# Float64 weights joined to float32 by integer operations instead of TensorE sums, and a planner with other step lengths and one booking for VectorE and GpSimd

## The chip, the cores and the metric

The kernel runs on one core of one Trainium2 chip. The metric is the device time of one execution in microseconds, lower is better; a kernel is run several times and its median is given. A profile is one further execution, recorded instruction by instruction.

## The reference

Three blocks follow each other. First an attention: `q` has 12288 rows of 128, `kv` is a 384 x 32 field of rows of 128 that is averaged over 4 x 4 patches to 768 rows and multiplied by `w_sr` (128 x 128); the same 768 rows are keys and values.

```
kv_pool = kv.reshape(B, H // r, r, W // r, r, C).mean(axis=(2, 4))
k = v = kv_pool.reshape(B, -1, C) @ w_sr
s = scale * (q @ k.transpose(0, 2, 1));  s = s - s.max(-1)
a = np.exp(s);  a /= a.sum(-1) + 1e-09;  x = a @ v
x = g1(x @ w_in1) @ w_out1      # g1(h) = h if h > 0 else exp(h) - 1
x = g2(x @ w_in2) @ w_out2      # g2(h) = max(0.01 h, h)
```

Both layers have 128 x 2048 weights in and 2048 x 128 weights out. The four weight matrices come as float64, everything else as float32.

## The kernel before

*Products.* Every large product is done with float32r operands in three passes (`mm3`, L88 to L91): a number is split in a head `hi` (the value rounded to float32r) and a tail `lo` (what is left), and hi x hi, hi x lo and lo x hi are summed in PSUM. So every operand needs a head, mostly made by ScalarE or GpSimd, and a tail, mostly a subtraction on VectorE.

*Stages.* The 12288 rows go in 24 chunks of 512. For each chunk, four tiles of 128 rows go through the attention: `scores` (TensorE), `largest` (VectorE, L343), `expo` (ScalarE, L350), `invert` (VectorE, L358 and L359), `norm` (GpSimd, L369), then the transposition of the probabilities, `head_e` (ScalarE, L414) and `tail_e` (VectorE, L418). In the first two chunks TensorE transposes (`turn_early`, L409); later ones go through DRAM (`send`, `fetch`, two transfers on SP) and a VectorE transpose (L398). `values` (L429) makes the chunk's attention output in 18 matmuls, `head_x` and `tail_x` (L437) split it. Then come the two layers in units of 256 of the 2048 hidden columns, 8 units a chunk and layer: `up` into a PSUM place, the activation, `tail` (L496), `down` into a sum `py`. Ten units of layer one run alone; then units of layer one and layer two alternate. At the start `kv` is loaded in 12 transfers and pooled (`column_sums` on VectorE, L283; `row_sums` on TensorE, L292).

*The weights.* The four matrices are cut into 16 parts of 128 x 512. Each is loaded as pairs of 32-bit words (`load_w`) into one of two `ws` buffers and made into a head and a tail that stay in SBUF (`w_parts`). Before the change a part goes through nine steps: ScalarE takes the absolute value of the high word read as float32 (`w_abs`, L197); GpSimd bounds it (`w_bound`, L201); VectorE shifts it left by 3 bits (`w_shift`, L208), which makes the float64 exponent a float32 one, puts sign and top bit back (`w_sign`, L215) and takes the power of two alone (`w_power`, L222). ScalarE rounds to the head (`w_head`, L228), VectorE scales the low word by the power of two (`w_b`, L233). Then TensorE sums in a PSUM place the float32 value times the identity (L240), minus the head (L241) and plus the low word's share (L242), and ScalarE copies that sum out as the tail (`w_tail`, L245), which frees the place. Four parts are due early, the others six units ahead of the unit that uses them.

*PSUM.* Three places of 128 x 1024 (`ps`) serve scores, early transposes, attention output, up products and weight sums in turn; two more are the sums `py`. A place is held from the first matmul of its use to the end of the last reader.

*The order of work.* Nothing is written in program order by hand. `step` registers each operation with its engine, an estimated length, what it comes after and a due key; `take` and `give` register buffers and PSUM places. A greedy planner then goes through time: of all steps that can begin it takes the one that begins first, ties within 0.25 us going to the lower key, and emits it. `LATE` is the delay after which another engine sees a result. The order in which a step is emitted is the order on its engine's queue; the engines work their queues in order and wait on semaphores.

Of the kernel before, what the change touches and what calls it, by code (L numbers as in the profile page):

```python
# [36 lines left out]
TOP = struct.unpack("f", struct.pack("I", 0x47EFFFFF))[0]  # L37
LEAST = struct.unpack("f", struct.pack("I", 0x38000000))[0]
# [3 lines left out]
def pooled_attention_elu_leaky_kernel(  # L42
# [55 lines left out]
    plus = const.tile([P, P], F32R, name="plus")  # L98
    minus = const.tile([P, P], F32R, name="minus")
# [23 lines left out]
    wt_p = pool("wt", 1)  # L123
# [61 lines left out]
    def w_parts(i):  # L185

        k, p = wjobs[i]  # L190
# [58 lines left out]

# [9 lines left out]
    nc.scalar.activation(out=plus, in_=ident, func=AF.Copy)  # L259
    nc.scalar.activation(out=minus, in_=ident, func=AF.Copy, scale=-1.0)  # L260
# [274 lines left out]
    def step(engine, length, do, after, key, size=0):  # L535
# [5 lines left out]
        steps.append((engine, length, do, [a for a in after if a is not None], key, size))  # L541
# [37 lines left out]
    for i in range(NL):  # L579
# [3 lines left out]
        cs = step(DVE, 0.7, lambda i=i: column_sums(i), [ld], key + 1)  # L583
        rs = step(PE, 0.5, lambda i=i: row_sums(i), [cs, previous], key + 1)
# [17 lines left out]
    for i, (k, p) in enumerate(wjobs):  # L602
# [29 lines left out]
    tq = step(DVE, 0.7, lambda: turn_q(0), first_q[:1], begin + 12)  # L632
# [259 lines left out]
```

## Time and profile before

| what | value |
| --- | --- |
| median of 3 runs | 1345.92 us (1345.49 to 1346.61) |
| span of the profiled execution, first to last instruction | 1343.9 us |
| what the median has beyond that span | 2.0 us |
| instructions in the profile | 16278 |
| mean granted TensorE clock | 0.994 |

The profiled execution is known by its span; the runs' times also hold what lies around the first and the last instruction. The views that are used are the page (busy times), the busy time of each engine by stretch, the chain of waits that ended last, the waits of an engine by releaser, groups of instructions by line, and the timeline. Times in them are counted from the span's start. L240 is line 240 of the kernel before. A matmul's recorded time overlaps its neighbour's, so distances between starts tell more than single durations.

### The profile page before, as it was taken

What the parts mean: (1) busy time and instruction counts of PE and PEld (TensorE: products, weight loads), DVE (VectorE), ACT (ScalarE), POOL (GpSimd) and SP (SyncE); (2) the same over time, 40 slices, a digit from 0 to 9 for tenths busy, and PEclk for the clock granted to TensorE, in tenths of its full rate; (3) what the DMA queues carried; (4) which work ended last, traced back from release to release, by engine and by line L of the source; (5) the groups of instructions that cost most, each with busy time, mean ns of one, the idle gap of its engine ahead of it and who ended that gap; (6) DMA issues with size and microseconds to landing.
All of it is one profiled execution on the core that took longest, in us unless ns stands there. A gap on an engine that the chain in (4) does not pass through costs nothing.

```text
span 1343.9 us, 16278 instructions
## 1 busy us (share of the span) xinstructions
PE 1311.5 (98%) x5848; PEld 1082.4 (81%) x5848; DVE 1102.8 (82%) x1259; ACT 993.2 (74%) x1197; POOL 377.6 (28%) x310
## 2 busy tenths in 40 slices
PE   7788999999999999999999999999999999999998
PEld 6566788888888888888888888888888888888886
DVE  5799987887887988978878878879889788788664
ACT  3667787787777787877877877777877778778675
POOL 0234332322222322323323232323223233233110
PEclk9999999999999999999999999999999999999999
DMA  9233322322223223223223132232232232222001
GB/s 276 56 110 88 101 67 67 87 55 79 72 54 94 57 55 90 76 55 87 55 79 86 54 81 67 55 89 65 55 87 71 63 87 55 71 79 55 0 9 16
DMA packets 169376, 97.60 MB, mean 73 GB/s; under 512 B 104656, under 2 KB 153936, under 8 KB 169296
## 3 DMA queue, kind: packets, MB, share of 16 engines
q1 hardware_dynamic: 168096, 96.36, 26.4%
q8 instruction: 47, 0.77, 0.2%
q10 hardware_dynamic: 1200, 0.20, 0.1%
q14 instruction: 33, 0.27, 0.1%
HBM read 55.64 MB, written 40.89 MB: 72 GB/s over the span
## 4 chain that ended last, share of the span: by engine, by line
PE 95%; DVE 3%; ACT 1%; issue 0%; DMA 0%; POOL 0%; DVEq 0%; ACTq 0%
PE ps L89 15%; PE ps L90 15%; PE ps L91 15%; PE py L90 13%; PE py L91 13%; PE py L89 13%; PE ps L429 7%; PE ps L240 1%; PE ps L292 1%; DVE nm L343 0%; DVE el L418 0%; DVE a L215 0%; DVE g L473 0%; DMA kv<-in_kv_dram 0%; PE ps L242 0%
## 5 line engine op out<-in xcount | busy, mean ns | idle before, releaser
L496 DVE TENSOR_TENSOR gl<-g,gh 128x1024 fp32r<-128x1024 f32 x384 | 469.7, 1247 | 77.8 <-POOL gh L482 63.5
L482 POOL TENSOR_SCALAR gh<-g 128x1024 fp32r<-128x1024 f32 x192 | 219.7, 1144 | 683.2 <-DVE g L473 670.2
L90 PE MATMUL py<-gl,wh_o 128*128 128x512 f32 x768 | 302.7, 394 | 2.9 <-DVE gl L496 2.9
L466 ACT ACTIVATE r<-ps 128x1024 f32<-128x1024 f32 x192 | 197.1, 1027 | 145.5 <-PE ps L91 145.4
L91 PE MATMUL py<-gh,wl_o 128*128 128x512 f32 x768 | 300.4, 391 | 0.0
L89 PE MATMUL py<-gh,wh_o 128*128 128x512 f32 x768 | 300.1, 391 | 0.0
L473 DVE SCALAR_TENSOR_TENSOR g<-r,ps 128x1024 f32<-128x1024 f32 x192 | 233.4, 1215 | 73.3 <-ACT r L469 70.0
L488 ACT ACTIVATE gh<-ps 128x1024 fp32r<-128x1024 f32 x192 | 196.8, 1025 | 55.7 <-PE ps L91 54.1
L469 ACT ACTIVATE r<-r 128x1024 f32<-128x1024 f32 x192 | 203.5, 1060 | 4.7
L492 ACT ACTIVATE g<-ps 128x1024 f32<-128x1024 f32 x192 | 196.4, 1023 | 0.0
L369 POOL TENSOR_SCALAR e<-e,rs 128x768 f32<-128x768 f32 x88 | 137.8, 1566 | 172.8 <-DVE rs L359 163.9
L91 PEld LDWEIGHTS py<-gh,wl_o 128*128 128x128 f32 x768 | 144.3, 188 | 31.2
L90 PEld LDWEIGHTS py<-gl,wh_o 128*128 128x128 f32 x768 | 144.2, 188 | 31.2 <-DVE gl L496 3.8
L89 PEld LDWEIGHTS py<-gh,wh_o 128*128 128x128 f32 x768 | 144.2, 188 | 29.5
L89 PE MATMUL ps<-xh,wh_i 128*128 128x512 f32 x384 | 150.5, 392 | 1.6 <-DVE el L418 0.9
L90 PE MATMUL ps<-x2l,wh_i 128*128 128x512 f32 x384 | 151.3, 394 | 0.0
L90 PE MATMUL ps<-xl,wh_i 128*128 128x512 f32 x384 | 151.0, 393 | 0.0
L89 PE MATMUL ps<-x2h,wh_i 128*128 128x512 f32 x384 | 150.6, 392 | 0.0
L91 PE MATMUL ps<-x2h,wl_i 128*128 128x512 f32 x384 | 150.1, 391 | 0.0
L91 PE MATMUL ps<-xh,wl_i 128*128 128x512 f32 x384 | 149.9, 390 | 0.0
L418 DVE TENSOR_TENSOR el<-e,eh 128x768 fp32r<-128x768 f32 x88 | 100.4, 1141 | 20.4 <-ACT eh L414 20.4
L350 ACT ACTIVATE e<-ps,nm 128x768 f32<-128x768 f32 x96 | 85.8, 894 | 36.5 <-DVE nm L343 28.8
(79 smaller groups left out, 1584.1 us busy)
## 6 DMA issues: line engine op xcount, KB each, us to landing
d<-e SPq DMA_DIRECT2D x88, 384.0 KB, 2.6
x<-d SPq DMA_DIRECT2D x88, 384.0 KB, 3.0
kv<-in_kv_dram SPq DMA_DIRECT2D x12, 512.0 KB, 6.1
qn<-in_q_dram SPq DMA_DIRECT2D x96, 64.0 KB, 3.6
out_dram<-y SPq DMA_DIRECT2D x94, 64.0 KB, 2.4
ws<-in_moe_w_in_dram SPq DMA_DIRECT2D x8, 512.0 KB, 3.9
ws<-in_moe_w_out_dram SPq DMA_DIRECT2D x8, 512.0 KB, 3.9
out_dram<-y ACTq DMA_DIRECT2D x2, 64.0 KB, 2.9
```

What stands on the lines that cost most here:

```text
L89: nc.tensor.matmul(ps, w_hi, x_hi, start=start, stop=False)
L90: nc.tensor.matmul(ps, w_hi, x_lo, start=False, stop=False)
L91: nc.tensor.matmul(ps, w_lo, x_hi, start=False, stop=stop)
L369: nc.gpsimd.tensor_scalar(out=x, in0=e, scalar1=rs_t.pop(t), scalar2=1.0, op0=ALU.mult, op1=ALU.mult)
L418: nc.vector.tensor_tensor(out=lo, in0=e_t.pop(t), in1=f(hi), op=ALU.subtract)
L466: nc.scalar.activation(out=r_u[n], in_=ps_u[n], func=AF.Relu, scale=-1.0)
L469: nc.scalar.activation(out=r_u[n], in_=r_u[n], func=AF.Exp, scale=-1.0)
L473: nc.vector.scalar_tensor_tensor(out=g_u[n], in0=r_u.pop(n), scalar=-1.0, in1=ps_u.pop(n), op0=ALU.add, op1=ALU.max)
L482: on.tensor_scalar(out=gh_u[n], in0=g_u[n], scalar1=1.0, scalar2=0.0, op0=ALU.mult, op1=ALU.add)
L488: nc.scalar.activation(out=gh_u[n], in_=ps_u[n], func=AF.Prelu, alpha=0.01)
L492: nc.scalar.activation(out=g_u[n], in_=ps_u.pop(n), func=AF.Prelu, alpha=0.01)
L496: nc.vector.tensor_tensor(out=gl_u[n], in0=g_u.pop(n), in1=f(gh_u[n]), op=ALU.subtract)
```

## The change

A weight part now goes through seven steps and no longer uses TensorE or a PSUM place. ScalarE scales the high word, read as float32, by 2^-112 (`w_scale`); GpSimd or VectorE, whichever the planner finds sooner, bounds it on both sides (`w_bound`). ScalarE turns the low word into an integer from 0 to 7 (`w_low`), with which the `ws` buffer is free. VectorE puts the sign bit into that integer (`w_sign`) and joins it with the scaled word shifted left by 3 (`w_join`): the result is the float32 value. ScalarE rounds it to the head as before (`w_head`), VectorE subtracts the head for the tail (`w_tail`). The temporary tiles are now `m` and `r`, two buffers each, instead of `m`, `a` and `b`, one each. The two scaled identities `plus` and `minus` go.

In the planner nearly all step lengths change, on VectorE and ScalarE mostly downwards (of the lines left out below, none changes by more than 0.4 us). `LATE` changes, and GpSimd steps start 0.1 us after they are ready (`START`). Steps marked `port=True`, on VectorE or GpSimd, are planned one after the other and never at once (`shared`). A scores step takes its PSUM place only when two are open (`"spare"`). The transpose of the next chunk's queries comes after the scores of the chunk's third tile (`mine[-2]`).

```diff
-TOP = struct.unpack("f", struct.pack("I", 0x47EFFFFF))[0]
-LEAST = struct.unpack("f", struct.pack("I", 0x38000000))[0]
+LOW = 7.499 * 2.0 ** -32
+TOP = struct.unpack("f", struct.pack("I", 0x0FEFFFFF))[0]
...
-        def w_abs():
-            wt[i] = {"m": wt_p.tile([P, WP], F32, tag="m", name="m")}
-            nc.scalar.activation(out=wt[i]["m"], in_=f(wst[i][:, :, 1]), func=AF.Abs)
-        def w_bound():
+        def new(tag, dtype=F32):
+            wt.setdefault(i, {})[tag] = wt_p.tile([P, WP], dtype, tag=tag, name=tag)
+            return wt[i][tag]
+        def w_scale(on):
+            nc.scalar.activation(
+                out=new("m"), in_=f(wst[i][:, :, 1]), func=AF.Copy, scale=2.0 ** -112
+            )
+        def w_bound(on):
             m = wt[i]["m"]
-            nc.gpsimd.tensor_scalar(
-                out=m, in0=m, scalar1=TOP, scalar2=LEAST, op0=ALU.min, op1=ALU.max
+            on.tensor_scalar(out=m, in0=m, scalar1=TOP, scalar2=-TOP, op0=ALU.min, op1=ALU.max)
+        def w_low(on):
+            nc.scalar.activation(
+                out=new("r", U32), in_=wst[i][:, :, 0], func=AF.Copy, scale=LOW
             )
-        def w_shift():
-            m, a = wt[i]["m"], wt_p.tile([P, WP], F32, tag="a", name="a")
-            wt[i]["a"] = a
-            nc.vector.tensor_scalar(
-                out=u(a), in0=u(m), scalar1=3, scalar2=0x3FFFFFF8,
-                op0=ALU.logical_shift_left, op1=ALU.bitwise_and,
-            )
-        def w_sign():
-            m, a = wt[i]["m"], wt[i]["a"]
+        def w_sign(on):
+            r = wt[i]["r"]
             nc.vector.scalar_tensor_tensor(
-                out=u(a), in0=wst[i][:, :, 1], scalar=0xC0000000, in1=u(a),
+                out=r, in0=u(wt[i]["m"]), scalar=0x80000000, in1=r,
                 op0=ALU.bitwise_and, op1=ALU.bitwise_or,
             )
-        def w_power():
-            m, a = wt[i]["m"], wt[i]["a"]
-            nc.vector.tensor_scalar(
-                out=u(m), in0=u(a), scalar1=0xFF800000, scalar2=None, op0=ALU.bitwise_and
+        def w_join(on):
+            m = u(wt[i]["m"])
+            nc.vector.scalar_tensor_tensor(
+                out=m, in0=m, scalar=3, in1=wt[i]["r"],
+                op0=ALU.logical_shift_left, op1=ALU.bitwise_or,
             )
-        def w_head():
-            a = wt[i]["a"]
-            nc.scalar.activation(out=hi, in_=a, func=AF.Copy)
-        def w_b():
-            m, b = wt[i]["m"], wt_p.tile([P, WP], F32R, tag="b", name="b")
-            wt[i]["b"] = b
-            nc.vector.scalar_tensor_tensor(
-                out=b, in0=wst[i][:, :, 0], scalar=2.0 ** -52, in1=m, op0=ALU.mult, op1=ALU.mult
-            )
-        def w_rest():
-            a, b = wt[i]["a"], wt[i]["b"]
-            ps = w_ps[i][:, 0, :WP]
-            nc.tensor.matmul(ps, ident, a, start=True, stop=False)
-            nc.tensor.matmul(ps, minus, hi, start=False, stop=False)
-            nc.tensor.matmul(ps, plus, b, start=False, stop=True)
-        def w_tail():
-            nc.scalar.activation(out=lo, in_=w_ps.pop(i)[:, 0, :WP], func=AF.Copy)
-        return w_abs, w_bound, w_shift, w_sign, w_power, w_head, w_b, w_rest, w_tail
+        def w_head(on):
+            nc.scalar.activation(out=hi, in_=wt[i]["m"], func=AF.Copy)
+        def w_tail(on):
+            on.tensor_tensor(out=lo, in0=wt[i]["m"], in1=f(hi), op=ALU.subtract)
+        return w_scale, w_bound, w_low, w_sign, w_join, w_head, w_tail
...
-    def step(engine, length, do, after, key, size=0):
+    def step(engine, length, do, after, key, size=0, port=False):
...
-        steps.append((engine, length, do, [a for a in after if a is not None], key, size))
+        steps.append((engine, length, do, [a for a in after if a is not None], key, size, port))
...
-        cs = step(DVE, 0.7, lambda i=i: column_sums(i), [ld], key + 1)
-        rs = step(PE, 0.5, lambda i=i: row_sums(i), [cs, previous], key + 1)
+        cs = step(DVE, 0.61, lambda i=i: column_sums(i), [ld], key + 1, port=True)
+        rs = step(PE, 0.9, lambda i=i: row_sums(i), [cs, previous], key + 1)
...
-        steps_w = w_parts(i)
-        ab = step(ACT, 0.65, steps_w[0], [ld], key)
-        bo = step(POOL, 1.0, steps_w[1], [ab], key)
-        sh = step(DVE, 0.6, steps_w[2], [bo], key + 0.1)
-        si = step(DVE, 0.7, steps_w[3], [sh], key + 0.2)
-        po = step(DVE, 0.6, steps_w[4], [si], key + 0.3)
-        hd = step(ACT, 0.65, steps_w[5], [si], key + 0.2)
-        wb = step(DVE, 0.7, steps_w[6], [po], key + 0.4)
-        wr = step(PE, 0.9, steps_w[7], [hd, wb], key + 0.5)
-        take(wr, "ps", None, 3, lambda ps, i=i: w_ps.__setitem__(i, ps))
-        wl = step(ACT, 0.65, steps_w[8], [wr], key + 0.6)
-        give(wl, "ps", wr)
-        for tag, begun, over in (("m", ab, wb), ("a", sh, wr), ("b", wb, wr)):
-            take(begun, tag, i, 1)
-            give(over, tag, i)
-        give(wb, "ws", i)
+        part = w_parts(i)
+        sc = step((ACT,), (0.58,), part[0], [ld], key)
+        bo = step((POOL, DVE), (0.72, 0.35), part[1], [sc], key, port=True)
+        lw = step((ACT,), (0.5,), part[2], [ld, sc], key + 0.05)
+        sg = step((DVE,), (0.6,), part[3], [bo, lw], key + 0.1, port=True)
+        jo = step((DVE,), (0.6,), part[4], [sg], key + 0.2, port=True)
+        hd = step((ACT,), (0.53,), part[5], [jo], key + 0.3)
+        wl = step((DVE,), (0.6,), part[6], [hd], key + 0.4, port=True)
+        take(sc, "wm", i, 2)
+        give(wl, "wm", i)
+        take(lw, "wr", i, 2)
+        give(jo, "wr", i)
+        give(lw, "ws", i)
...
-            take(s0, "ps", None, 3, lambda ps, t=t: sc_t.__setitem__(t, ps))
+            take(s0, "ps", "spare", 3, lambda ps, t=t: sc_t.__setitem__(t, ps))
...
-            mx = step(DVE, 1.03, lambda t=t: largest(t), [s1], key + 0.5)
-            xp = step(ACT, 1.0, lambda t=t: expo(t), [mx], key + 1)
+            mx = step(DVE, 0.87, lambda t=t: largest(t), [s1], key + 0.5)
+            xp = step(ACT, 0.875, lambda t=t: expo(t), [mx], key + 1)
...
-            iv = step(DVE, 0.35, lambda t=t: invert(t), [xp], key + 1.5)
-            no = step(POOL, 0.93, lambda t=t: norm(t), [iv], key + 2)
+            iv = step(DVE, 0.22, lambda t=t: invert(t), [xp], key + 1.5)
+            no = step(POOL, 0.95, lambda t=t: norm(t), [iv], key + 2, port=True)
...
-            he = step(ACT, 0.77, lambda t=t: head_e(t), [tu, av_done.get(c - 1)], key + 6)
-            te = step(DVE, 1.0, lambda t=t: tail_e(t), [he], key + 6.5)
+            he = step(ACT, 0.735, lambda t=t: head_e(t), [tu, av_done.get(c - 1)], key + 6)
+            te = step(DVE, 0.87, lambda t=t: tail_e(t), [he], key + 6.5, port=not early)
...
-            tq = step(DVE, 0.7, lambda c=c: turn_q(c + 1), [ld], end + 1)
+            tq = step(DVE, 0.63, lambda c=c: turn_q(c + 1), [ld, mine[-2]], end + 1)
...
-            re = step(ACT, 0.95, lambda n=n: relu(n), [u1, chain["act"]], n + 0.5)
-            xe = step(ACT, 1.05, lambda n=n: elu_exp(n), [re], n + 0.5)
-            el = step(DVE, 1.3, lambda n=n: elu(n), [xe], n + 1)
-            gh = step(POOL, 1.1, lambda n=n: elu_head(n, nc.gpsimd), [el], n + 1.5)
+            re = step(ACT, 0.92, lambda n=n: relu(n), [u1, chain["act"]], n + 0.5)
+            xe = step(ACT, 0.966, lambda n=n: elu_exp(n), [re], n + 0.5)
+            el = step(DVE, 1.135, lambda n=n: elu(n), [xe], n + 1)
+            gh = step(POOL, 1.08, lambda n=n: elu_head(n, nc.gpsimd), [el], n + 1.5, port=True)
...
-        tl = chain["tail"] = step(DVE, 1.25, lambda n=n: tail(n), [*both, chain["tail"]], n + 2)
+        tl = chain["tail"] = step(DVE, 1.135, lambda n=n: tail(n), [*both, chain["tail"]], n + 2, port=True)
...
-    LATE = {ACT: 0.2, DVE: 0.1, POOL: 0.15, PE: 0.25, SP: 3.0}
+    LATE = {ACT: 0.14, DVE: 0.12, POOL: 0.05, PE: 0.2, SP: 3.0}
+    START = {ACT: 0.0, DVE: 0.0, POOL: 0.1, PE: 0.0, SP: 0.0}
+    shared = 0.0
...
-                if not open_:
+                if len(open_) < (2 if n == "spare" else 1):
...
-                t = max(t, ready[i], free_at[e])
+                t = max(t, ready[i] + START[e], free_at[e])
+                if steps[i][6]:
+                    t = max(t, shared)
...
+        if port:
+            shared = end
```

## Rows read from the trace of the kernel before

**Rows 1.** The page: engine, busy us (share of the span), instructions.

```profile
PE 1311.5 (98%) x5848; PEld 1082.4 (81%) x5848; DVE 1102.8 (82%) x1259; ACT 993.2 (74%) x1197; POOL 377.6 (28%) x310
```

**Rows 2.** Stretches: us; PE, PEld, DVE, ACT, POOL busy (instructions); clock, DMA share, GB/s.

```profile
0.00:31.00 31.00, 21.29 (x128) 18.17 (x128) 17.49 (x36) 9.84 (x27) 1.93 (x8) 0.94 1.00 298
31.00:64.00 33.00, 23.82 (x115) 18.32 (x115) 25.46 (x46) 18.59 (x34) 7.91 (x10) 0.95 0.22 57
64.00:121.00 57.00, 49.80 (x199) 35.86 (x199) 51.38 (x66) 42.09 (x59) 23.81 (x21) 0.97 0.31 95
121.00:169.00 48.00, 47.93 (x196) 37.78 (x197) 45.43 (x57) 35.17 (x46) 17.13 (x13) 0.96 0.35 97
250.00:1198.00 948.00, 947.78 (x4241) 790.61 (x4240) 798.39 (x887) 724.04 (x851) 276.22 (x218) 1.00 0.26 71
```

**Rows 3.** The chain that ended last, by time: start us, us, what.

```profile
255.45 4.13 PE ps L429 x18
...
1197.52 4.12 PE ps L429 x18
```

**Rows 4.** Stretches, L240 alone: us; PE, PEld busy (instructions); clock, DMA.

```profile
31.00:64.00 33.00, 4.22 (x6) 1.10 (x6) 0.95 0.22 57
64.00:121.00 57.00, 7.61 (x12) 1.99 (x12) 0.97 0.31 95
121.00:169.00 48.00, 5.21 (x10) 1.80 (x10) 0.96 0.35 97
```

**Rows 5.** TensorE's waits, 31 to 121 us: us in total, times, longest.

```profile
PE ps L240 <- DVE ss L358: 3.8, 1, 3.8
PE ps L89 <- DVE el L418: 2.7, 3, 0.9
```

**Rows 6.** Timeline, TensorE from 133 us: start, us, line, operation [idle before].

```profile
133.21 1.02 PE L240 MATMUL ps<-a,ident 128*128 128x512 f32 x2
...
134.52 0.40 PE L89 MATMUL py<-gh,wh_o 128*128 128x512 f32 x1
```

**Rows 7.** Timeline, TensorE from 24 us.

```profile
24.30 1.02 PE L240 MATMUL ps<-a,ident 128*128 128x512 f32 x2
...
25.62 2.84 PE L292 MATMUL ps<-pool_m,s 128*128 128x128 f32 x24
```

**Rows 8.** Timeline, all engines, from 43 us.

```profile
43.98 2.08 PE L240 MATMUL ps<-a,ident 128*128 128x512 f32 x2 [3.77 <-DVE ss L358]
...
46.70 1.41 PE L409 MATMUL ps<-ident,x 128*128 128x128 f32 x11
...
47.73 0.91 POOL L369 TENSOR_SCALAR x<-e,rs 128x768 f32<-128x768 f32 x1 [2.46 <-PE ps L409]
```

**Rows 9.** Timeline, TensorE from 61 us.

```profile
61.73 1.02 PE L240 MATMUL ps<-a,ident 128*128 128x512 f32 x2
...
63.90 0.50 PE L89 MATMUL ps<-xh,wh_i 128*128 128x512 f32 x1 [0.69 <-ACT wl_i L245]
```

**Rows 10.** Groups, VectorE from 64 to 121 us, then whole span: busy, mean ns.

```profile
L215 DVE SCALAR_TENSOR_TENSOR a<-ws,a 128x512 uint32<-128x512 uint32 x6 | 5.5, 909 | 0.2
L233 DVE SCALAR_TENSOR_TENSOR b<-ws,m 128x512 fp32r<-128x512 uint32 x6 | 4.1, 678 | 0.2
...
L208 DVE TENSOR_SCALAR a<-m 128x512 uint32<-128x512 uint32 x5 | 3.6, 719 | 0.7 <-PE ps L242 0.5 <-PE ps L240 0.2
L222 DVE TENSOR_SCALAR m<-a 128x512 uint32<-128x512 uint32 x6 | 3.3, 545 | 0.1
...
L159 DVE TENSOR_TENSOR ql<-e,qh 128x512 fp32r<-128x512 f32 x24 | 16.5, 689 | 0.0
...
L197 ACT ACTIVATE m<-ws 128x512 f32<-128x512 f32 x16 | 10.7, 667 | 5.6 <-DVE b L233 5.5
```

**Rows 11.** Timeline, VectorE at 312 us and TensorE at 323 us.

```profile
312.52 0.69 DVE L437 TENSOR_TENSOR xl<-ps,xh 128x512 fp32r<-128x512 f32 x1 [0.84 <-ACT xh L433]
...
323.72 0.39 PE L89 MATMUL ps<-xh,wh_i 128*128 128x512 f32 x1
```

More of the change, by code (lines that the diff above doesn't have):

```diff
@@ L97, in pooled_attention_elu_leaky_kernel @@
     ident = const.tile([P, P], F32, name="ident")
-    plus = const.tile([P, P], F32R, name="plus")
-    minus = const.tile([P, P], F32R, name="minus")
     w_src = {"i1": w_in1, "o1": w_out1, "i2": w_in2, "o2": w_out2}
@@ L593, in pooled_attention_elu_leaky_kernel @@
             pr = step(PE, 0.5, lambda g=g: project(g), [cp], key + 2)
-            hk = step(ACT, 0.5, kv_step(g, head_kv), [pr], key + 3)
-            tk = step(DVE, 0.62, kv_step(g, tail_kv), [hk], key + 3)
+            hk = step(ACT, 0.35, kv_step(g, head_kv), [pr], key + 3)
+            tk = step(DVE, 0.4, kv_step(g, tail_kv), [hk], key + 3)
             give(tk, "ps", place_step)
@@ L611, in pooled_attention_elu_leaky_kernel @@
         take(ld, "ws", i, WS)
-        steps_w = w_parts(i)
-        ab = step(ACT, 0.65, steps_w[0], [ld], key)
-        bo = step(POOL, 1.0, steps_w[1], [ab], key)
-        sh = step(DVE, 0.6, steps_w[2], [bo], key + 0.1)
-        si = step(DVE, 0.7, steps_w[3], [sh], key + 0.2)
-        po = step(DVE, 0.6, steps_w[4], [si], key + 0.3)
-        hd = step(ACT, 0.65, steps_w[5], [si], key + 0.2)
-        wb = step(DVE, 0.7, steps_w[6], [po], key + 0.4)
-        wr = step(PE, 0.9, steps_w[7], [hd, wb], key + 0.5)
-        take(wr, "ps", None, 3, lambda ps, i=i: w_ps.__setitem__(i, ps))
-        wl = step(ACT, 0.65, steps_w[8], [wr], key + 0.6)
-        give(wl, "ps", wr)
-        for tag, begun, over in (("m", ab, wb), ("a", sh, wr), ("b", wb, wr)):
-            take(begun, tag, i, 1)
-            give(over, tag, i)
-        give(wb, "ws", i)
+        part = w_parts(i)
[11 more added lines that the diff above has]
+        give(lw, "ws", i)
         w_ready[k, p] = wl
     x_ready = {}
-    tq = step(DVE, 0.7, lambda: turn_q(0), first_q[:1], begin + 12)
+    tq = step(DVE, 0.63, lambda: turn_q(0), first_q[:1], begin + 12)
     take(tq, "e", ("q", 0), 3)
     give(tq, "qn", 0)
-    hq = step(ACT, 0.52, lambda: head_q(0), [tq], begin + 12)
-    tl = step(DVE, 0.65, lambda: tail_q(0), [hq], begin + 12)
+    hq = step(ACT, 0.53, lambda: head_q(0), [tq], begin + 12)
+    tl = step(DVE, 0.6, lambda: tail_q(0), [hq], begin + 12, port=True)
     give(tl, "e", ("q", 0))
@@ L669, in pooled_attention_elu_leaky_kernel @@
                 give(no, "e", ("e", t))
-                tu = step(PE, 0.66, lambda t=t: turn_early(t, ex.pop(t)), [no], key + 2.5)
+                tu = step(PE, 0.6, lambda t=t: turn_early(t, ex.pop(t)), [no], key + 2.5)
                 take(tu, "ps", None, 3, lambda ps, t=t: ex.__setitem__(t, ps))
@@ L679, in pooled_attention_elu_leaky_kernel @@
                 give(fe, "d", ("d", t))
-                tu = step(DVE, 1.0, lambda t=t: turn(t), [fe, av_done.get(c - 1)], key + 5.5)
+                tu = step(DVE, 0.9, lambda t=t: turn(t), [fe, av_done.get(c - 1)], key + 5.5)
                 take(tu, "e", ("t", t), 3)
                 give(tu, "x", ("x", t))
-            he = step(ACT, 0.77, lambda t=t: head_e(t), [tu, av_done.get(c - 1)], key + 6)
-            te = step(DVE, 1.0, lambda t=t: tail_e(t), [he], key + 6.5)
+            he = step(ACT, 0.735, lambda t=t: head_e(t), [tu, av_done.get(c - 1)], key + 6)
+            te = step(DVE, 0.87, lambda t=t: tail_e(t), [he], key + 6.5, port=not early)
             give(te, *(("ps", tu) if early else ("e", ("t", t))))
@@ L693, in pooled_attention_elu_leaky_kernel @@
                 take(ld, "qn", c + 1, 2)
-            tq = step(DVE, 0.7, lambda c=c: turn_q(c + 1), [ld], end + 1)
+            tq = step(DVE, 0.63, lambda c=c: turn_q(c + 1), [ld, mine[-2]], end + 1)
             take(tq, "e", ("q", c + 1), 3)
             give(tq, "qn", c + 1)
-            hq = step(ACT, 0.52, lambda c=c: head_q(c + 1), [tq, *mine], end + 1.2)
-            q_ready[c + 1] = step(DVE, 0.65, lambda c=c: tail_q(c + 1), [hq], end + 1.4)
+            hq = step(ACT, 0.53, lambda c=c: head_q(c + 1), [tq, *mine], end + 1.2)
+            q_ready[c + 1] = step(DVE, 0.6, lambda c=c: tail_q(c + 1), [hq], end + 1.4, port=True)
             give(q_ready[c + 1], "e", ("q", c + 1))
@@ L706, in ended @@
             del et[c]
-        hx = step(ACT, 0.52, lambda c=c: (et.pop(c), head_x(c)), [a1], end + 9)
-        x_ready[1, c] = step(DVE, 0.72, lambda c=c: tail_x(c), [hx], end + 9.2)
+        hx = step(ACT, 0.5, lambda c=c: (et.pop(c), head_x(c)), [a1], end + 9)
+        x_ready[1, c] = step(DVE, 0.61, lambda c=c: tail_x(c), [hx], end + 9.2)
         take(hx, "xs", c, 2)
@@ L732, in pooled_attention_elu_leaky_kernel @@
         else:
-            lh = step(ACT, 0.95, lambda n=n: leaky_head(n), [u1, chain["act"]], n + 0.5)
-            lk = step(ACT, 0.95, lambda n=n: leaky(n), [lh], n + 0.5)
+            lh = step(ACT, 0.92, lambda n=n: leaky_head(n), [u1, chain["act"]], n + 0.5)
+            lk = step(ACT, 0.905, lambda n=n: leaky(n), [lh], n + 0.5)
             chain["act"] = lk
@@ L743, in pooled_attention_elu_leaky_kernel @@
         d0 = step(
-            PE, 0.69, lambda n=n: down(n, 0), [tl, w_ready[f"o{m}", 2 * P * u // WP], chain["down"]],
+            PE, 0.687, lambda n=n: down(n, 0), [tl, w_ready[f"o{m}", 2 * P * u // WP], chain["down"]],
             n + LAG[m],
         )
-        d1 = chain["down"] = step(PE, 0.69, lambda n=n: down(n, 1), [d0], n + LAG[m])
+        d1 = chain["down"] = step(PE, 0.687, lambda n=n: down(n, 1), [d0], n + LAG[m])
         if u == 0:
@@ L752, in pooled_attention_elu_leaky_kernel @@
         if u == NU - 1 and m == 1:
-            hx = step(ACT, 0.55, lambda c=c: head_x2(c), [d1], n + LAG[m] + 0.3)
-            x_ready[2, c] = step(DVE, 0.72, lambda c=c: tail_x2(c), [hx], n + LAG[m] + 0.4)
+            hx = step(ACT, 0.5, lambda c=c: head_x2(c), [d1], n + LAG[m] + 0.3)
+            x_ready[2, c] = step(DVE, 0.61, lambda c=c: tail_x2(c), [hx], n + LAG[m] + 0.4)
             take(hx, "x2", c, 2)
@@ L757, in pooled_attention_elu_leaky_kernel @@
         elif u == NU - 1:
-            ty = step(DVE, 0.75, lambda c=c: turn_y(c), [d1], n + LAG[m] + 2)
+            ty = step(DVE, 0.64, lambda c=c: turn_y(c), [d1], n + LAG[m] + 2)
             take(ty, "y", c, 1)
@@ L829, in pooled_attention_elu_leaky_kernel @@
         _, t, e, i = best
-        engines, lengths, do, _, key, size = steps[i]
+        engines, lengths, do, _, key, size, port = steps[i]
         length = lengths[engines.index(e)]
```

10 lines of the change are left out of this document (4 added, 6 removed).

## The prediction

> **What bounds the kernel now.** I read the busy times first. TensorE is busy 1311.5 of 1343.9 us, VectorE 1102.8 [rows 1], so TensorE sets the pace on average. An average hides stages, so the next view is the same table by stretch [rows 2]. From 250 to 1198 us TensorE is busy 947.78 of 948 us: no other engine can shorten that part. In the chain of waits the attention products of successive chunks (18 matmuls each) start at 255.45 and 1197.52 us, 18 chunks apart [rows 3], so one chunk takes 942.07 / 18 = 52.34 us, all of it TensorE. What can still move is the front. TensorE idles 9.7 us in the first 31 us, 9.2 us from 31 to 64, 7.2 us from 64 to 121, and almost nothing from 121 to 169 [rows 2]. There the sixteen weight parts are made: L240 has two records a part, so 3, 6 and 5 parts fall in the last three of these stretches [rows 4] and two in the first. From 64 to 121 us VectorE is busy 51.38 of 57 us and TensorE 49.80, so two engines are near their limit; from 121 to 169 us it is 45.43 and 47.93 of 48.
>
> TensorE's waits between 31 and 121 us name the weight parts themselves: the longest, 3.8 us, is that of L240 behind VectorE's L358 [rows 5]. L358 does not make its operand. It stands beside the release of a PSUM place, of which there are three for scores, early transposes, attention output, up products and weight sums alike. So a weight part costs TensorE its matmuls and also its turn in the queue while it waits for a place.
>
> **What the change removes, and what it costs.** At full clock one part takes TensorE from 133.21 to 134.52 us, 1.31 us [rows 6]; sixteen take 21.0 us. They vanish, and with them one PSUM place per part from L240 to the end of the tail, L245. What that is worth I work out by stretch.
>
> *0 to 31 us, two parts.* The second begins at 24.30 us, and 24 pooling matmuls stand right behind it at 25.62 us [rows 7]; without it they begin 1.3 us earlier. Of the first I count nothing: data is still landing then. I take 1.3 us; the bounds are 0 (the loads set the end) and 2 x 1.31 = 2.6.
>
> *31 to 64 us, three parts.* At 43.98 us L240 had waited 3.77 us for its place, then the part ran until 46.70 us, the transposes of two attention tiles behind it, and GpSimd's next tile waited 2.46 us for those transposes [rows 8]. Later the first up product waits for the part that begins at 61.73 us and starts at 63.90, 2.17 us on, the last 0.69 of them a wait for that part's tail, whose exit frees the place [rows 9]. I take 2.46 + 2.17 = 4.6 us. The low bound is the second alone, 2.2. The high one takes both whole, the wait in front of the first too, and the third part at full clock: 3.77 + 2.72 + 2.17 + 1.31 = 10.0 us.
>
> *64 to 121 us, six parts.* TensorE would give back 6 x 1.31 = 7.9 us. But VectorE is as full and has to follow. Before, a part took it 0.909 + 0.678 + 0.719 + 0.545 = 2.85 us in this stretch. After, it has three passes: sign, join and the new tail, a subtraction where ScalarE did a copy. They are 128x512 passes with two SBUF inputs, as are L159, 0.689 us, and L215 here, 0.909 us [rows 10]. Three of the first kind make 2.07 us and save 0.78 us a part, 4.7 us in six; three of the second make 2.73 and save 0.12 a part, 0.7 us. I take 4.7, since the plan now books VectorE and GpSimd apart, between 0.7 and 7.9.
>
> The gap between 0.689 and 0.909 us is passes that met GpSimd. The Trainium skill (SBUF — State Buffer, section "SBUF: two separate sides") says that a VectorE operation with two SBUF inputs and a GpSimd operation that reads SBUF take one port pair by an exclusive lock, and the later one waits for the whole of the other. By that rule all three new passes are exposed, where of the old four two had two such inputs; with each at 0.909 us this term is 0.7 and not 4.7 us, and the sum below 15.2 and not 19.2. L233, with two SBUF inputs in the same stretch, has a mean of 0.678 us [rows 10], so the trace does not show that every such pass pays.
>
> *121 to 169 us, five parts.* TensorE does not wait here [rows 2], so each part counts whole: 5 x 1.31 = 6.6 us. The low bound is VectorE's, 5 x 0.12 = 0.6 us, should its 95% become the limit. I take 6.6, since its attention work can be put off: in the steady state the attention output is ready at 312.52 + 0.69 = 313.21 us and first used at 323.72, 10.5 us later [rows 11].
>
> *ScalarE and GpSimd.* ScalarE loses abs and the copy out of PSUM and gains scale and the low word, both strided reads like L197, 0.667 us [rows 10]. Were that copy free, it would gain 0.667 us a part, 4.0 us in six, against 14.9 us idle from 64 to 121 [rows 2]. I cost it at nothing; without that cover it would be those 0.667 us a part. GpSimd's bound stays one pass, or goes to VectorE where the plan finds that sooner. The two identity copies that go come before the first data lands; nothing.
>
> *The plan.* Step lengths, delays and the shared booking change the order on every engine. No row prices that. The largest wait left that is not a weight part's is that of the scores behind L418, 2.7 us in three [rows 5]; with other lengths part of such waits can go. I take 2.0, between 0 and 2.7. Two rules can delay: a scores step must now find two open places, and a query's transpose stands behind the scores of its chunk's third tile. Behind the scores are queued L343 on VectorE, L350 on ScalarE, L369 on GpSimd and, on SP, the two transfers of the tile; the reserve of 10.5 us pays for them.
>
> Sum: 1.3 + 4.6 + 4.7 + 6.6 + 2.0 = 19.2 us. The profiled span of 1343.9 us becomes 1324.7. The median of the runs shown, 1345.92 us, is 2.0 us above the span; with the same around it I expect 1326.7 us. The low bounds sum to 3.5 us (1342.4), the high ones to 29.8 us (1316.1).
>
> **Rivals.**
> *VectorE takes over.* For it: 51.38 of 57 and 45.43 of 48 us busy. The stretches from 64 to 169 us then give only 0.7 to 4.7 and 0.6 to 5 x 0.78 = 3.9 us, and with the first two at 0 and 2.2 the gain is 3.5 to 10.8 us: about 1338 us. Against it: its attention work is done 10.5 us ahead of need.
>
> *More than the matmuls.* With places free the terms come near their high bounds: a gain of 25 to 30 us, about 1318 us. For it: the 3.8 us wait at L240 [rows 5]. Against it: the VectorE share.
>
> *The clock falls more often.* The two L240 at 43.98 us took 2.08 us, those at 133.21 us 1.02 [rows 6, 8]: behind the wait of 3.77 us TensorE ran at the lower level, 1.2 GHz. The granted clocks of the first four stretches, 0.94, 0.95, 0.97 and 0.96 [rows 2], put the time lost at that level near 0.06 x 31 + 0.05 x 33 + 0.03 x 57 + 0.04 x 48 = 7.1 us. The weight matmuls also kept TensorE going between attention steps; if without them such stretches double, 7 us are lost again: about 1334 us. The Trainium skill (TensorE: Matmul & The Clock Gate, section "HAM oscillation — how this bites in real kernels") says that an engine left waiting between bursts is gated down again. By that rule the removal works against itself in the front; the trace agrees that a fall followed a wait, but a wait for the weight part's own place.
>
> *Slower: attention falls behind in the steady state.* The second open place that scores now ask for is where it would begin. Up to 10.5 us of delay cost nothing; beyond, every chunk's first up product waits and TensorE idles. At 19.2 / 22 = 0.9 us in each of 22 chunks the gain is gone; at 1.2 us it ends at 1326.7 + 26.4 = 1353 us. For it: TensorE has no idle time there to hide a wait. Against it: 10.5 us is a fifth of a chunk.
>
> *Nothing.* What the front gains turns into other waits there: 1346 us.
>
> **How the numbers follow.** The forecast as summed (own range 1321 to 1332) 0.49; more than the matmuls 0.17; VectorE takes over 0.15; the clock 0.05; slower 0.09; nothing 0.05. The range from 1315, a microsecond past the high bounds, to 1339 leaves out slower, nothing and a little of the VectorE case. A measurement of this kernel can tell 0.2%, 2.7 us, from no change; faster is 0.49 + 0.17 + 0.15 + 0.05 = 0.86, same 0.05, slower 0.09.
>
> **What would show it.** L240 to L242 gone from TensorE, the period still 52.3 us, the whole difference in place by 170 us. By steps: the pooling matmuls end about 1 us earlier, the first up product starts 4 to 6 us before 63.90, the weight passes on VectorE take near 0.69 us, TensorE has no wait from 121 us on. Wrong: a period over 52.5 us, an up product waiting for attention output, more half-clock stretches than before, or a first up product at 63 us or later.

## The result and the profile after

The changed kernel takes 1330.25 us (median of 4 runs, 1329.19 to 1331.06) beside 1346.05 us before (the three runs of the table and one more): a ratio of 0.9881, 95% interval 0.9867 to 0.9895, 15.8 us less. The forecast was 1326.7 us. The profiled execution has a span of 1328.6 us.

The page, busy times, and the busy times by stretch, which answer to [rows 1, 2]:

```profile
PE 1290.8 (97%) x5784; PEld 1070.4 (81%) x5784; DVE 1083.8 (82%) x1246; ACT 1004.1 (76%) x1195; POOL 357.2 (27%) x307
```

```profile
0.00:31.00 31.00, 19.74 (x126) 17.35 (x127) 17.35 (x38) 10.63 (x28) 1.31 (x7) 1.00 1.00 299
31.00:64.00 33.00, 24.37 (x125) 20.02 (x124) 29.53 (x51) 27.00 (x45) 12.07 (x14) 0.95 0.36 104
64.00:121.00 57.00, 47.77 (x194) 37.24 (x193) 49.64 (x61) 41.60 (x56) 22.48 (x20) 0.88 0.34 99
121.00:169.00 48.00, 45.37 (x197) 35.89 (x195) 45.32 (x54) 39.14 (x51) 15.88 (x13) 1.00 0.26 75
250.00:1198.00 948.00, 947.81 (x4245) 791.06 (x4245) 790.00 (x888) 735.35 (x852) 261.96 (x218) 1.00 0.27 71
```

5848 - 5784 = 64 matmul records are gone, four for each part, and with them 1311.5 - 1290.8 = 20.7 us of TensorE's busy time. Its idle time rose from 32.4 to 37.8 us, so the span is 15.3 us shorter. From 250 us on TensorE is as full as before. What is new stands from 64 to 169 us: TensorE idles 9.2 + 2.6 us there (7.2 + 0.1 before), and the granted clock from 64 to 121 us is 0.88 where it was 0.97.

The chain by time, the attention products of two chunks 17 apart (compare [rows 3]):

```profile
294.92 4.12 PE ps L406 x18
...
1183.66 4.12 PE ps L406 x18
```

888.74 / 17 = 52.28 us a chunk, where it was 52.34: the steady state is nearly what it was, and gives about 1 us over all chunks. The rest of the difference was made before 250 us.

The timeline of TensorE at the first scores and at the first up product; the first row is the kernel before, which answers to the second, and the third answers to [rows 9]:

```profile
31.25 0.44 PE L89 MATMUL ps<-kt_hi,qh 128*128 128x384 f32 x1 [0.37 <-ACT kt_hi L316]
```

```profile
29.65 0.44 PE L89 MATMUL ps<-kt_hi,qh 128*128 128x384 f32 x1 [0.36 <-ACT kt_hi L293]
...
53.99 0.51 PE L89 MATMUL ps<-xh,wh_i 128*128 128x512 f32 x1 [0.60 <-DVE xl L414]
```

The scores begin 1.6 us earlier, the first up product 9.9 us. That product does not measure the lead, because the order of the other work changed as well. The work done does: without the weight sums, four records a part in 2, 3, 6 and 5 parts, TensorE has 6, 22, 19 and 21 matmuls more than before in the four stretches up to 169 us (a matmul across a border counts on both sides). Counted by their starts in the two traces, each at the distance between starts that its kind has in a full pipeline at the upper clock (0.23 us for 512 columns, 0.17 for 384, 0.11 for 128), TensorE gained an estimated 1.0, 4.2, 4.5 and 4.3 us of work in them, 14.1 by 169 us, and nothing more by 250 us.

That is less than the 21 us of the sums. TensorE's waits from 31 to 121 us (compare [rows 5]) and the queue of VectorE in front of the longest of them show a part of the loss:

```profile
PE py L90 <- DVE gl L473: 7.6, 2, 5.6
PE ps L386 <- POOL x L346: 4.1, 2, 3.8
PE ps L89 <- DVE el L395: 1.7, 2, 1.2
```

```profile
100.17 0.95 DVE L395 TENSOR_TENSOR el<-e,eh 128x768 fp32r<-128x768 f32 x1
101.34 0.96 DVE L320 TENSOR_REDUCE nm<-ps 128x1 f32<-128x768 f32 x1 [0.22 <-PE ps L91]
102.21 1.28 DVE L210 SCALAR_TENSOR_TENSOR r<-m,r 128x512 uint32<-128x512 uint32 x2
103.41 1.29 DVE L217 SCALAR_TENSOR_TENSOR m<-m,r 128x512 uint32<-128x512 uint32 x2
104.79 0.69 DVE L226 TENSOR_TENSOR wl_o<-m,wh_o 128x512 fp32r<-128x512 f32 x1
105.40 0.69 DVE L226 TENSOR_TENSOR wl_i<-m,wh_i 128x512 fp32r<-128x512 f32 x1
106.00 1.22 DVE L473 TENSOR_TENSOR gl<-g,gh 128x1024 fp32r<-128x1024 f32 x1
```

```profile
107.28 0.79 PE L90 MATMUL py<-gl,wh_o 128*128 128x512 f32 x1 [5.55 <-DVE gl L473]
```

Six passes of two weight parts stand in VectorE's queue in front of the tail `gl` that a down product needs; TensorE waits 5.55 us. The same table for that place alone, with the clock third from the end:

```profile
99.40:113.00 13.60, 8.05 (x21) 6.18 (x21) 12.43 (x15) 6.67 (x10) 5.56 (x5) 0.50 0.22 77
```

For 13.6 us the clock is at its lower level, 1.2 GHz. TensorE is busy 8.05 us of them, which at the upper level would have been near 4.0: 4 us lost, beside the waits. Another wait ends just before:

```profile
97.17 0.50 PE L90 MATMUL py<-gl,wh_o 128*128 128x512 f32 x1 [2.10 <-DVE gl L473]
```

But the kernel before lost no less at that level. These are its four stretches there, and then the other one of the changed kernel:

```profile
16.00:19.50 3.50, 3.50 (x11) 2.47 (x12) 1.92 (x3) 0.95 (x2) 0.61 (x1) 0.51 1.04 391
43.40:46.80 3.40, 2.82 (x5) 1.49 (x6) 1.67 (x6) 0.14 (x2) 0.90 (x1) 0.50 0.86 163
70.70:74.10 3.40, 3.14 (x6) 1.82 (x7) 2.62 (x4) 1.69 (x3) 2.76 (x3) 0.50 0.58 196
121.90:125.30 3.40, 3.40 (x10) 2.87 (x9) 3.37 (x7) 0.85 (x1) 1.71 (x2) 0.50 0.34 54
```

```profile
37.90:41.30 3.40, 3.40 (x14) 3.07 (x12) 1.99 (x7) 2.28 (x5) 1.79 (x2) 0.50 0.78 192
```

At half the clock half of the busy time is lost: 12.86 / 2 = 6.4 us before and (8.05 + 3.40) / 2 = 5.7 us after.

The passes themselves came out as taken. Groups of the changed kernel, mean ns after the bar (compare [rows 10]):

```profile
L210 DVE SCALAR_TENSOR_TENSOR r<-m,r 128x512 uint32<-128x512 uint32 x16 | 11.3, 722 | 1.3 <-ACT r L204 1.2
L217 DVE SCALAR_TENSOR_TENSOR m<-m,r 128x512 uint32<-128x512 uint32 x16 | 10.9, 695 | 0.1
...
L226 DVE TENSOR_TENSOR wl_i<-m,wh_i 128x512 fp32r<-128x512 f32 x8 | 5.5, 686 | 0.3 <-ACT wh_i L223 0.2
```

0.722 + 0.695 + 0.686 = 2.10 us a part; the forecast took 2.07.

### The profile page after: what moved, and what is told of

Read it like the earlier page. It is cut to its first block, busy times and chain, and to the rows that moved or that the text cites. A ratio compares the mean times of both kernels' runs of the same rounds, so it can differ in the third digit from the quotient of the medians.

```text
span 1328.6 us, 16081 instructions
## 1 busy us (share of the span) xinstructions
PE 1290.8 (97%) x5784; PEld 1070.4 (81%) x5784; DVE 1083.8 (82%) x1246; ACT 1004.1 (76%) x1195; POOL 357.2 (27%) x307
## 4 chain that ended last, share of the span: by engine, by line
PE 93%; DVE 4%; ACT 2%; issue 1%; DMA 0%; POOL 0%; DVEq 0%; ACTq 0%; POOLq 0%
PE ps L91 15%; PE ps L90 15%; PE ps L89 15%; PE py L91 13%; PE py L90 13%; PE py L89 13%; PE ps L406 7%; PE ps L269 1%; DVE gl L473 1%; DVE g L450 1%; DVE nm L320 0%; ACT e L327 0%; DVE m L217 0%; DVE r L210 0%; DVE el L395 0%
## 5 line engine op out<-in xcount | busy, mean ns | idle before, releaser
L459 POOL TENSOR_SCALAR gh<-g 128x1024 fp32r<-128x1024 f32 x192 | 230.9, 1203 | 603.4 <-DVE g L450 487.0
L450 DVE SCALAR_TENSOR_TENSOR g<-r,ps 128x1024 f32<-128x1024 f32 x192 | 231.3, 1207 | 50.9 <-ACT r L446 48.4
L346 POOL TENSOR_SCALAR e<-e,rs 128x768 f32<-128x768 f32 x88 | 107.5, 1221 | 256.1 <-ACT r L443 120.5
L320 DVE TENSOR_REDUCE nm<-ps 128x1 f32<-128x768 f32 x96 | 91.8, 957 | 40.7 <-PE ps L91 39.1
```

Source lines behind the costliest of these rows:

```text
L346: nc.gpsimd.tensor_scalar(out=x, in0=e, scalar1=rs_t.pop(t), scalar2=1.0, op0=ALU.mult, op1=ALU.mult)
L450: nc.vector.scalar_tensor_tensor(out=g_u[n], in0=r_u.pop(n), scalar=-1.0, in1=ps_u.pop(n), op0=ALU.add, op1=ALU.max)
L459: on.tensor_scalar(out=gh_u[n], in0=g_u[n], scalar1=1.0, scalar2=0.0, op0=ALU.mult, op1=ALU.add)
```

## The experiments

Two theories stood at the start. *V*: VectorE is what the front waits for, its queue decides what the freed time of TensorE is worth. *T*: TensorE's own time counts whole, and the loss comes from the new order of scores and places. Times below are medians; ratios are against the kernel before on the same chip. The diffs are shortened and stand against the changed kernel, which is called *after*.

**e1: the weights alone.** The new `w_parts` and its seven steps in the planner of before.

```diff
-        sg = step((DVE,), (0.6,), part[3], [bo, lw], key + 0.1, port=True)
+        sg = step((DVE,), (0.6,), part[3], [bo, lw], key + 0.1)
...
-    LATE = {ACT: 0.14, DVE: 0.12, POOL: 0.05, PE: 0.2, SP: 3.0}
+    LATE = {ACT: 0.2, DVE: 0.1, POOL: 0.15, PE: 0.25, SP: 3.0}
```

> The seven-step weights in the planner of before (old lengths, old delays, no shared booking, no rule for scores or queries). Theory W, the weight steps carry the gain as the forecast had it (17.2 of 19.2 us): about 1346 - 16 = 1330 us, 1327 to 1333. Rival, the plan carries a good part of it: 1335 us or more. Without the shared booking GpSimd's norm (1.566 us before, 1.221 after) should stay near 1.5 us.

Measured: 1332.68 us, ratio 0.9888 (0.9873 to 0.9902). The weight steps alone carry the gain; what after has over it lies inside the intervals. GpSimd's norm, at 1.588 us, came as expected. The gain is made at other times than in after: counted as above, TensorE gains 2.1, -0.9, 6.3 and 5.3 us of work in the four stretches. From 31 to 64 us the clock is at 0.79, where before and after have 0.95, and the first up product starts only 1.5 us before that of the kernel before:

```profile
31.00:64.00 33.00, 22.35 (x98) 18.27 (x96) 28.02 (x48) 22.43 (x40) 10.55 (x11) 0.79 0.44 111
64.00:121.00 57.00, 46.62 (x203) 35.97 (x204) 52.28 (x64) 42.73 (x57) 26.19 (x21) 1.00 0.28 86
```

```profile
62.40 0.40 PE L89 MATMUL ps<-xh,wh_i 128*128 128x512 f32 x1
```

**e8: the plan alone.** The old nine-step weights, with their sums on TensorE, in the new planner without the rule of two places for scores.

```diff
-        part = w_parts(i)
-        sc = step((ACT,), (0.58,), part[0], [ld], key)
+        steps_w = w_parts(i)
+        ab = step(ACT, 0.65, steps_w[0], [ld], key)
...
-                if len(open_) < (2 if n == "spare" else 1):
+                if len(open_) < 1:
```

> The nine-step weights of before with TensorE's sums, in the planner of after but for the rule for scores (with it the old weights find no order). If the planner's part is small (the forecast took 2.0 us of 19.2): 1341 to 1347 us. Rival, the planner carries as much as the weights: 1335 us or less. With e1 at a ratio of 0.989 and after at 0.988, the sum of both alone would then exceed what both together give.

Measured: 1345.73 us, ratio 1.0002 (0.9992 to 1.0011). The planner alone shows no gain; the 2.0 us of the forecast are not there.

**e3, e4: one rule of the planner left out.**

```diff
-                if steps[i][6]:
-                    t = max(t, shared)
```

> After without the shared booking of VectorE and GpSimd in the planner. Theory V with collisions: the norm on GpSimd goes back from 1.22 to about 1.5 us, the passes of VectorE that meet it grow, and the time is 1328 to 1336 us. Rival, the booking only makes the plan leave VectorE empty while GpSimd works: without it 1318 to 1324 us.

```diff
-                if len(open_) < (2 if n == "spare" else 1):
+                if len(open_) < 1:
```

> After without the rule that scores must find two open places. Theory V: within 3 us of 1330, since places are not what TensorE waits for any more. Rival, the rule holds the attention back in the front: 1322 to 1327 us. The rule as a guard of the steady state (the slower rival of the forecast): a period over 52.5 us a chunk without it, 1336 us or more.

Measured: without the booking 1330.51 us, ratio 0.9873 (0.9859 to 0.9888), as after. Without the rule for scores 1323.52 us, ratio 0.9831 (0.9808 to 0.9854), about 6.7 us better than after. Here V, which expected no change, missed, and the rival came true: the rule holds the attention back in the front, so the order of scores, the second half of T, has a price. By the pages TensorE is busy 3.5 us less than in after and idle 3.2 us less (busy 1287.3 of a span of 1321.9). VectorE shows how that may come about. The busy times from 54 to 150 us, after, then e3, then e4 (third number behind the length: VectorE):

```profile
54.00:150.00 96.00, 82.68 (x345) 64.73 (x346) 86.84 (x108) 74.59 (x101) 35.99 (x32) 0.93 0.30 89
```

```profile
54.00:150.00 96.00, 84.13 (x356) 65.42 (x357) 94.68 (x114) 76.43 (x104) 40.82 (x33) 0.96 0.35 99
```

```profile
54.00:150.00 96.00, 84.92 (x367) 67.25 (x368) 90.91 (x116) 79.29 (x106) 37.95 (x33) 0.98 0.34 99
```

With earlier scores VectorE works 4 us more in the same stretch at nearly the same length of its passes (`gl` 1.255 us beside 1.258), and 22 more matmuls of TensorE begin in it. In e3 VectorE is busier still, 94.68 us, but part of that is longer passes:

```profile
L217 DVE SCALAR_TENSOR_TENSOR m<-m,r 128x512 uint32<-128x512 uint32 x16 | 14.9, 944 | 0.2
L210 DVE SCALAR_TENSOR_TENSOR r<-m,r 128x512 uint32<-128x512 uint32 x16 | 13.5, 852 | 1.3 <-ACT r L204 1.2
```

0.944 and 0.852 us against 0.695 and 0.722: the booking does shorten the weight passes, as the forecast took it. That the time stays the same fits a plan that pays for them with idle time of VectorE; it was not tested apart. The expected price, GpSimd's norm back at 1.5 us, did not come: it is 1.292 us.

**e2, e11: one pass less for VectorE.** The subtraction for a part's tail may go to GpSimd; e11 leaves out the rule for scores too.

```diff
-        wl = step((DVE,), (0.6,), part[6], [hd], key + 0.4, port=True)
+        wl = step((POOL, DVE), (1.0, 0.6), part[6], [hd], key + 0.4, port=True)
```

> After, and the subtraction that makes a weight part's tail may go to GpSimd or to VectorE, as the planner finds it sooner. Theory V, VectorE stands in the way from 64 to 169 us (weight passes ahead of the activations' tails): eleven parts less one pass of 0.69 us each are up to 7.6 us of VectorE, and the time falls by 3 to 8 us, to 1322 to 1327. Rival, TensorE's waits there come from the order of the scores or from places: within 2 us of 1330. If the port that both engines use is the limit, moving a pass from one to the other gives nothing either.

> After without the rule of two open places for scores (e4) and with the tail of a weight part on GpSimd or VectorE (e2). If the two take away different waits their gains of about 5 and 7 us add: 1317 to 1320 us. If both only shorten what VectorE holds up between 54 and 150 us, the better one is nearly all: 1321 to 1325 us.

Measured: 1326.12 us, ratio 0.9841 (0.9826 to 0.9856), about 5 us better than after, as V had it, with 13 of the 16 subtractions on GpSimd. Together 1324.12 us, ratio 0.9848 (0.9829 to 0.9866): the two gains do not add, as expected if both shorten the same waits.

**e5, e6: VectorE's weight passes shortened, or one of them doubled, in the same order.** e5 leaves 448 of 512 columns of each part unjoined.

```diff
-                out=r, in0=u(wt[i]["m"]), scalar=0x80000000, in1=r,
+                out=r[:, :64], in0=u(wt[i]["m"])[:, :64], scalar=0x80000000, in1=r[:, :64],
...
-                out=m, in0=m, scalar=3, in1=wt[i]["r"],
+                out=m[:, :64], in0=m[:, :64], scalar=3, in1=wt[i]["r"][:, :64],
```

> After with the same order of instructions on every engine; the sign and the join of each weight part work on 64 of 512 columns, so 448 columns of every part's weights are left unjoined. VectorE loses about 1 us a part. Theory V, the weight passes in front of the activations' tails in VectorE's queue are what TensorE waits for: most of its 9.5 us of waits at L90 from 97 us on go, and part of the half-clock stretch of 99 to 113 us with them: 1316 to 1323 us. Rival, those waits end on GpSimd's heads or on a PSUM place: within 2 us of 1330.

e6 issues the sign pass a second time:

```diff
+            nc.vector.scalar_tensor_tensor(
+                out=r, in0=u(wt[i]["m"]), scalar=0x80000000, in1=r,
+                op0=ALU.bitwise_and, op1=ALU.bitwise_or,
+            )
```

> After with the same order; the sign pass of each weight part is done twice, which changes no value: 16 times 0.6 us more on VectorE, eleven of them behind 64 us. Theory V: VectorE has little room there, 6.6 us or more show and some half-clock time with them: 1335 to 1341 us. Rival, VectorE's 13.6 us of idle time from 31 to 169 us take it in: within 2 us of 1330.

Measured: doubled, 1344.62 us, ratio 0.9981 (0.9970 to 0.9992): 14 us for 16 x 0.6 = 9.6 us of VectorE, past what V expected. Its ten runs fall in two groups, three from 1340.4 to 1340.7 and seven from 1344.5 to 1345.0 us, so the price is 10 us or 14. The trace is of the first group: TensorE idles 8.2 us more than in after and is busy 1.9 us more (1292.7 of 1338.7). What the second group adds has no trace. Shortened, 1326.73 us, ratio 0.9860 (0.9844 to 0.9877): 3.5 us for some 15 us of VectorE, less than V said, and the interval meets that of after. In the shortened kernel the waits of TensorE from 54 to 150 us still stand behind the tails:

```profile
PE py L90 <- DVE gl L473: 7.9, 3, 4.8
```

So VectorE's load is not the whole of it: with the order kept, its queue then waits more on others, for scores (4.0 us in after) and for the head `wh_o` of ScalarE:

```profile
DVE nm L320 <- PE ps L91: 6.0, 6, 1.5
DVE wl_o L226 <- ACT wh_o L223: 2.6, 4, 1.1
```

From 54 to 150 us VectorE is busy 81.36 us and idle 14.6, where it idled 9.2 in after.

**e9: the order at that one place.** The passes of the tenth and eleventh part are held until the tail of unit 8 is queued.

```diff
+        if i in (9, 10):
+            held.append(sg)
...
+        if n == 8:
+            for a in held:
+                steps[a][3].append(tl)
```

> After, and the passes of the tenth and eleventh weight part on VectorE are held until the tail of unit 8 is in VectorE's queue: that tail then stands in front of the six passes instead of behind them. Theory O, the order at that one place costs the 5.5 us wait at 107 us and the half-clock time behind it: 1320 to 1325 us. Theory L, VectorE has more work by then than time, and whatever is put behind is waited for later: the wait of 5.5 us shrinks, another one grows, and the time stays within 3 us of 1330.

Measured: 1328.93 us, ratio 0.9883 (0.9865 to 0.9901), the same as after. The waits of TensorE on the tails, 54 to 150 us, in e9 and in after:

```profile
PE py L90 <- DVE gl L473: 6.6, 4, 2.2
```

```profile
PE py L90 <- DVE gl L473: 9.5, 4, 5.6
```

The wait of 5.55 us is gone, and two stand in its place:

```profile
103.86 0.79 PE L90 MATMUL py<-gl,wh_o 128*128 128x512 f32 x1 [1.75 <-DVE gl L473]
...
108.79 0.50 PE L90 MATMUL py<-gl,wh_o 128*128 128x512 f32 x1 [2.01 <-DVE gl L473]
```

Theory O falls: the place in the queue was not the cause, VectorE is late by then whichever goes first.

**e7: TensorE's time put back.**

```diff
+        if n < 16 and i == 0:
+            for _ in range(6):
+                nc.tensor.matmul(ps_u[n][:, i, :], wh, xin[m, c][0], start=True, stop=True)
```

> After with the same order; each of the first 16 units makes six extra matmuls of 128x512 into its own PSUM place in front of its up product, 1.37 us a unit, 22.0 us in all, about what the weight sums took; nothing else changes. Theory T, TensorE's time counts whole: 1330 + 22 = 1352 us. Theory V, TensorE waits 13.3 us for VectorE's work between 54 and 136 us and runs at half clock for 13.65 us of it, so a good part goes into those waits: 1338 to 1345 us.

Measured: 1344.73 us, ratio 0.9990 (0.9981 to 0.9999), 14.5 us for 22.0 us of matmuls, so T's whole count falls and V's range holds. TensorE is busy 19.4 us longer than in after and idle 4.8 us less (busy 1310.2 of 1343.2): a third goes into waits that are there anyway and into a better clock, from 64 to 121 us 0.94 where after has 0.88.

```profile
64.00:121.00 57.00, 50.33 (x222) 41.05 (x221) 47.23 (x59) 36.13 (x50) 20.78 (x20) 0.94 0.32 94
```

**e10: the new lengths without the three rules** (no booking, no two places, no query transpose behind scores).

```diff
-                if steps[i][6]:
-                    t = max(t, shared)
...
-                if len(open_) < (2 if n == "spare" else 1):
+                if len(open_) < 1:
...
-            tq = step(DVE, 0.63, lambda c=c: turn_q(c + 1), [ld, mine[-2]], end + 1)
+            tq = step(DVE, 0.63, lambda c=c: turn_q(c + 1), [ld], end + 1)
```

> After with the new step lengths and delays but without the three rules that came with them: no shared booking, no two open places for scores, no query transpose behind the scores. The slower rival of the forecast, here without its guards: the attention or the ups lose time in every chunk, a period over 52.9 us and 1340 us or more (0.6 us in each of 22 chunks). Otherwise, as the booking and the places rule each alone cost nothing to leave out: the period stays 52.3 us and the time is 1320 to 1332 us.

Measured: 1399.27 us, ratio 1.0406 (1.0381 to 1.0431). The attention products of chunks 18 apart, and from 250 to 1198 us TensorE's largest wait and the busy times:

```profile
243.90 0.74 PE L406 MATMUL ps<-eh,v_hi 128*128 128x512 f32 x2
...
1258.45 0.51 PE L406 MATMUL ps<-eh,v_hi 128*128 128x512 f32 x1 [0.64 <-ACT g L469]
```

```profile
PE ps L89 <- DVE g L450: 26.2, 24, 2.1
```

```profile
250.00:1198.00 948.00, 918.44 (x3975) 739.48 (x3974) 746.32 (x832) 679.50 (x797) 246.88 (x204) 0.99 0.25 67
```

1014.55 / 18 = 56.4 us a chunk, 4 us more than in after: a steady state that TensorE no longer fills. It waits for the PSUM place that `elu` frees (L450), in front of up products, not for attention output. These waits are 26.2 of the 29.6 us that it idles there; 4 us in each of some 17 chunks are near 70, and what makes up the rest was not found.

## Why the prediction came out as it did

The direction, the place (14.1 of 15.3 us by 169 us) and the size within the range were right; 15.8 us came of 19.2. That the weight steps give it and not the planner is shown by e1 and e8.

*Removal of TensorE's sums.* Right that 21 us of matmuls go: TensorE is busy 20.7 us less. Too high was the term for 121 to 169 us, where five parts were to count whole because TensorE did not wait there: in after it idles 2.6 us, and an estimated 4.3 us came of 6.6. In e7, where such time was put back in front of up products, two thirds of it counted.

*By stretch,* in the work counted above: 1.0 us of 1.3 forecast, 4.2 of 4.6, 4.5 of 4.7 and 4.3 of 6.6. About 1 us came in the steady state, where nothing was forecast, and nothing shows for "the plan", 2.0 us: alone it has a ratio of 1.0002, and after and e1 cannot be told apart. So the division was near, but in part by luck. The 4.6 us of the second stretch were built of waits, and 2.46 of them were a wait of GpSimd's; TensorE's own idle time there fell only from 9.2 to 8.6 us, and three parts' own matmuls, 3 x 1.31 = 3.9 us, are about what came. With the old order (e1) the same stretches give -0.9 and 6.3 us in the second and third: where the gain falls depends on the order and on where the clock is low.

*VectorE takes over* was the nearest rival, and its mechanism is there in part: one more pass costs 10 to 14 us, one pass moved away gives 5, an order swapped gives none. Its price was too high. From 64 to 169 us it left 1.3 to 8.6 us, and an estimated 8.8 came, just past the upper end, which is that of passes of 0.69 us; the passes took 0.70 us as the forecast had it and not 0.91. In the first two stretches, where it took 0 and 2.2 us, 1.0 and 4.2 came. That the forecast's other sum, 15.2 us with passes of 0.909 us, is near the measured gain is chance: the passes did not take that long. The Trainium skill (SBUF — State Buffer, section "SBUF: two separate sides") has a VectorE pass with two SBUF inputs wait, by a lock, for a GpSimd pass that reads SBUF. By that rule the weight passes lengthen when nothing keeps them apart; the trace of e3 agrees, with 0.852 and 0.944 us. The forecast's reading of the old passes was too narrow, though: L208, with one SBUF input, grew as well when it met GpSimd, to 1.27 us in the kernel before where its shortest take 0.41:

```profile
72.99 1.95 POOL L482 TENSOR_SCALAR gh<-g 128x1024 fp32r<-128x1024 f32 x1
73.95 1.27 DVE L208 TENSOR_SCALAR a<-m 128x512 uint32<-128x512 uint32 x1
```

So the 2.85 us that an old part took already held such meetings in all its passes but L233.

*The clock* fell again, in fewer and longer stretches: 0.88 instead of 0.97 from 64 to 121 us. Over all stretches 5.7 us are lost at the lower level where it was 6.4, so the shortfall is not there, and the doubling that this rival feared did not come. The Trainium skill (TensorE: Matmul & The Clock Gate, section "HAM oscillation — how this bites in real kernels") ties such falls to waits between bursts of matmuls. By that rule the fall at 99.4 us belongs to VectorE's lateness; the trace agrees, since it comes behind a wait of 2.1 us that ends at 97.2 us, and it lasts through the one of 5.55.

*More than the matmuls* was in part to be had: e4 reaches 1323.52 us. The scores' second place, called a risk for the steady state, costs its price in the front instead.

*Slower* did not come. e10 shows that it is a real state of this planner once the rules are all gone. The waits found there are for a PSUM place for the up product, not for the late attention that the forecast named.

*Of the signs* the period, the earlier end of the pooling (1.6 us, as for the scores) and passes near 0.69 us came. The first up product moved 9.9 us and not 4 to 6, and TensorE does wait from 121 us on.

Open: how the loss divides between VectorE's load, the chain through its queue and the order of scores (e5 and e6 against e4), and which of the three rules e10 misses (the one for the query transpose was not left out alone); neither was tried further.

## What to carry to other kernels

Work taken off the engine that is 98% busy was worth 15 of its 21 us here, in part because a second engine near its limit came late with results (e2, e6): read the busy times stretch by stretch, and ask what the second engine has queued in front of the results that the first one needs. A swap of the order at the longest wait moved the wait. When the order changes too, the start of one product is no measure of the lead, 9.9 us beside some 5 us of work gained by 64 us: count the work done. And a planner's step lengths and its reservation rules are one thing: the booking and the rule for scores could each be left out alone, all three rules left out together made the changed kernel 5% slower.

## What the runs showed of the hardware

One pass more per weight part on VectorE (9.6 us) lengthened the kernel by 10 us in three runs and by 14 in seven. In the changed kernel the granted clock was 0.50 from 99.4 to 113.0 us, behind a wait of TensorE of 2.1 us and through one of 5.55; the 8.05 us that it was busy there would have been near 4.0 at the upper level. A weight pass of VectorE (128x512, two SBUF inputs) took 0.695 and 0.722 us in the mean when the plan booked it apart from GpSimd and 0.944 and 0.852 when it did not. The mean of the norm on GpSimd (128x768) was 1.566 us before, 1.221 after, 1.588 in e1, 1.292 in e3 without the booking and 1.534 in e4 with it. What sets it was not tested; e4, the fastest of these kernels, has one of the longer ones.
